# TensorE's order in a step of attention: scores, transposes, mixing, values

## The chip, the cores and the metric

The kernel runs on one core of one Trainium2 chip. The metric is the device time of one execution in microseconds (us), from the start of the program to its end. A core has a matrix engine (TensorE, PE in the rows), a vector engine (VectorE, DVE), an engine for functions of one argument (ScalarE, ACT), a general engine (GpSimd, POOL) and an engine that issues transfers (SyncE, SP). Each works through its own list of instructions and waits on semaphores for the others. PEld in the rows is TensorE's loading of the operand that stays in the array.

## What is computed

Attention with a bias made by a small network from the positions, then a dense layer with a softmax, a normalisation and a second matrix, then a mixture of eight experts with two experts per token. Only the attention is touched:

```python
def _attn_ref(q, k, v, w1, b1, w2):            # B 2, H 8, S 576, D 64; hidden 32
    scores = scale * np.matmul(q, k.transpose(0, 1, 3, 2))
    x = (psi_rel / psi_i)[..., None]           # from the positions alone
    h = np.maximum(x @ w1 + b1, 0.0)
    bias = h @ w2
    scores = scores + bias.transpose(2, 0, 1)[None]
    scores = scores - np.max(scores, axis=-1, keepdims=True)
    attn = np.exp(scores)
    attn = attn / (np.sum(attn, axis=-1, keepdims=True) + 1e-09)
    return np.matmul(attn, v)
```

## The kernel before

Attention is cut into 40 pieces A[k]: five tiles of queries (`it`, four of 128 rows and a last one of 64), four pairs of heads (`hp`) and two batches (`b`), with `b` running fastest. Two pieces that differ in `b` alone are a unit (`it`, `hp`); an even k is batch 0 of a unit, an odd k batch 1. A loop over k = 0, 1, 2, ... makes one step of each; what one piece needs is spread over several steps.

- **Scores**, `qk(k)` (L302, L306 for the last tile): TensorE multiplies queries and keys of two heads into two pairs of banks named `d`, one pair for each head. VectorE then adds the bias tile `bt`, which was brought from memory, and takes the extreme of each row in one instruction for each head (L311, output `e` and `nm`); it frees the bank. ScalarE takes the exponential of each head and the row sums (L318, output `e` and `sums`).
- **Transposes**, `tr(k - 2)` (LAG is 2): TensorE transposes `e` of the piece two steps back, eight blocks into one `d` (L330) and the remainders into `rest` (L332). ScalarE copies the blocks out (L333, output `et`), and for batch 1 the remainders of both batches (L335). For batch 1, VectorE makes the reciprocals `rs` of the sums (L337, L338), and GpSimd spreads them to `rb` (L341).
- **Values**, `av`: TensorE transposes `rb` (L353) and multiplies `et` with the values (L362) into the one bank `av`. ScalarE copies the product out (L365), VectorE multiplies it with the reciprocals (L366, output `XA`). Before, this is done for both batches of a unit at once, in every even step.
- **Mixing**, `bias_step` (L203): TensorE mixes 0/1 masks `mk` into the bias of positions that later pieces need, 16 matmuls into each of two `d`; VectorE frees them (L208 and L209) and SyncE stores the result. The masks are made by GpSimd (five of eight) and VectorE (three of eight) at L191. Twelve of the 36 mixing steps lie ahead of the loop, one in each step k = 0 to 23, none later.
- **Conversions**: the weights `w_in` and `w_out` come as 64-bit numbers, and from about step 20 on ScalarE (L252, L258), VectorE (L253, L255 to L257) and GpSimd (L253, L259) turn them into pairs of 32-bit numbers, in the gaps of attention.

There are three `d` (of two banks each); `rest` and `av` have one bank each. A step with mixing uses five `d`: one for transposes, two for scores, two for mixing. So each use waits until the use three before it has been emptied.

The program text gives the order of work; a scheduler then places each instruction on its engine's list by its own estimate of when operands are ready, so instructions can stand ahead of or behind their place in the text. On one engine nothing is reordered after that.

Of the kernel before, what the change touches and what calls it, by code (L numbers as in the profile page):

```python
# [9 lines left out]
F32 = mybir.dt.float32  # L10
# [10 lines left out]
B, H, S, D = 2, 8, 576, 64  # L21
# [5 lines left out]
JB = 5  # L27
# [5 lines left out]
LAG = 2  # L33
# [38 lines left out]
def _build(tc, nc, ctx, I, O):  # L72
# [267 lines left out]
                u.rb = ap.tile([128, 4, 64], F32, name="rb", bufs=2)  # L340
                P_.tensor_copy(u.rb, u.rs[:, :, None].to_broadcast([128, 4, 64]))  # L341

    def av(it, hp):

        u = SU.pop((it, hp))
        n = 128 if it < 4 else 64
        o = psum.tile([128, 2, 256], F32, name="av").rearrange("p w (b i) -> p w b i", b=2)
        for b in range(B):
            for x in range(2):
                h = slice(64 * x, 64 * x + 64)  # L350
                if n == 128:
                    if x == 0:
                        nc.tensor.transpose(o[:, 1, b], u.rb[:, 2 * b:2 * b + 2].rearrange("p x d -> p (x d)"), ident)  # L353
                else:
                    nc.tensor.matmul(o[h, 1, b, 0:64], u.rs[h, b:b + 1].to_broadcast([64, 64]), ident[h, h],
                                     start=True, stop=True)
        for b in range(B):
            v = KV[hp, b][:, S:].rearrange("p (j d) -> p j d", j=JB)
            for jb in range(JB):
                for x in range(2):  # L360
                    w = u.et[:, 2 * b + x, jb] if n == 128 else u.et[:, b, jb, 64 * x:64 * x + 64]
                    nc.tensor.matmul(o[64 * x:64 * x + 64, 0, b, 0:n], v[:, jb, 64 * x:64 * x + 64], w,  # L362
                                     start=(jb == 0), stop=(jb == JB - 1))
        dst = XA[:, it:it + 5:4, hp] if n == 128 else XA[:, 8, hp].rearrange("p (b i) -> p b i", b=2)
        nc.scalar.activation(dst, o[:, 0, :, 0:n], AF.Copy)  # L365
        V.tensor_tensor(out=dst, in0=dst, in1=o[:, 1, :, 0:n], op=OP.mult)  # L366
# [9 lines left out]
    for k in range(len(A) + LAG + 8):  # L376
        if k % 2 == 0 and k < len(A):
            bias_in(k // 2 + 2)
        if k % 8 == 6 and k // 8 + 1 < 5:
            load_q(k // 8 + 1)  # L380
        if LAG <= k < len(A) + LAG:
            tr(*A[k - LAG])
        if LAG <= k - 1 < len(A) + LAG and A[k - 1 - LAG][2] == 1:
            av(*A[k - 1 - LAG][:2])
        if k < len(A):
            qk(*A[k])
        bias_step(2 * PRE + k)
        if k == CONV[0] - 10:
            raws = [fetch_in(*c) for c in chunks[:RB64]]
        if k in CONV:  # L390
# [543 lines left out]
```

## Time and profile before

| | us |
|---|---|
| median of 3 runs | 640.64 |
| lowest and highest run | 640.61, 641.03 |
| the profiled execution | 641.07 |
| its span, first to last instruction | 639.3 |

The times of rows below are of the profiled execution and count from the start of its span. The masks and the first mixing steps take it to about 35 us; attention's loop then runs to about 237 us; the dense layer and the experts follow and are not touched. PEclk is the TensorE clock that was granted, as a share of full speed: 1.00 is 2.4 GHz and 0.50 is 1.2 GHz. In brackets behind an instruction stands how long its engine was idle just before it, and which instruction ended that wait. Instructions of one line that follow each other are merged, with their number behind the x; two on one engine can overlap by up to a tenth of a microsecond or so, since each is shown until its result has landed.

### The profile page before, as it was taken

The numbers are of one execution on the slowest core, as the hardware profiler recorded it, in microseconds if no ns is written. First come the engines' busy times: TensorE is split into PE (matmuls) and PEld (weight loads), VectorE is DVE, ScalarE is ACT, GpSimd is POOL, SyncE is SP. The second block draws the span as 40 slices with busy tenths as digits, with TensorE's granted clock in tenths as the row PEclk, the third lists the DMA queues.
The fourth block names the chain that finished last, engine by engine and source line by source line (L and its number), as shares of the span: only waits on it lengthen the run. The fifth ranks groups of instructions, "written<-read, shape, count | busy, mean of one in ns | idle before, by whom it ended". The sixth has DMA issues, their size and how long they took to land. (4 is left out here: it accounts for less than half of the span.)

```text
span 639.3 us, 12768 instructions
## 1 busy us (share of the span) xinstructions
PE 582.0 (91%) x5068; PEld 475.9 (74%) x5068; DVE 392.2 (61%) x909; ACT 341.9 (53%) x657; POOL 232.9 (36%) x177
## 2 busy tenths in 40 slices
PE   0879999998789999999999989999999999999990
PEld 0546777776567878678888788888898989898980
DVE  4988777777873336983546788774646474543400
ACT  6934656566675665663436436554545454544410
POOL 4999998973230017420000302322222121222111
PEclk9979999999989999999999999999999999999996
DMA  8794524317441015200312334757565656636212
GB/s 314 275 328 145 208 87 183 112 38 266 164 156 48 1 42 204 74 19 32 106 59 91 108 122 160 255 139 216 162 199 182 184 194 162 224 64 191 35 19 29
DMA packets 33945, 89.45 MB, mean 140 GB/s; under 512 B 3601, under 2 KB 5137, under 8 KB 33873
## 3 DMA queue, kind: packets, MB, share of 16 engines
q1 hardware_dynamic: 26480, 72.04, 31.3%
q0 software_dynamic: 5808, 13.37, 10.3%
q10 hardware_dynamic: 1584, 3.11, 1.3%
q8 instruction: 42, 0.69, 0.4%
q14 instruction: 31, 0.25, 0.1%
HBM read 67.66 MB, written 20.84 MB: 138 GB/s over the span
## 5 line engine op out<-in xcount | busy, mean ns | idle before, releaser
L191 POOL TENSOR_SCALAR mk<-T,thr 128x576 bf16<-128x576 f16 x67 | 116.9, 1759 | 13.0 <-PE d L203 8.9
L804 PE MATMUL phe<-xgt,wp 128*128 128x320 f32 x768 | 115.9, 310 | 2.3 <-ACT xgt L402 2.3
L804 PEld LDWEIGHTS phe<-xgt,wp 128*128 128x128 f32 x768 | 113.2, 188 | 3.0 <-ACT xgt L402 2.5
L638 POOL DMA_INDIRECT out<-y,si x24 | 39.6, 1652 | 149.5 <-ACT y L794 72.6
L787 PE MATMUL poe<-wp,hT 128*128 128x512 f32 x384 | 90.9, 393 | 0.0
L787 PEld LDWEIGHTS poe<-wp,hT 128*128 128x128 f32 x384 | 71.0, 188 | 14.1
L318 ACT ACTIVATE e<-e,nm 128x576 f32<-128x576 f32 x72 | 55.4, 771 | 42.5 <-DVE nm L311 42.4
L203 PE MATMUL d<-mk,wd 128*32 128x288 bf16 x1152 | 48.7, 302 | 26.9 <-POOL wd L170 14.2
L203 PEld LDWEIGHTS <-wd 128*32 128x32 f16 x1152 | 29.9, 100 | 47.3 <-issue 23.6
L311 DVE CUSTOM_DVE_ANT_0 e<-d,bt 128x576 f32<-128x576 f32 x72 | 52.2, 755 | 19.7 <-PE d L302 13.8
L807 DVE SCALAR_TENSOR_TENSOR hT<-phe,hT 128x320 fp32r<-128x320 f32 x64 | 31.3, 489 | 50.2 <-ACT hT L806 49.7
L302 PE MATMUL d<-kv,q 64*128 64x288 f32 x256 | 51.0, 447 | 5.7 <-DVE nm L311 5.2
L403 DVE TENSOR_TENSOR wp<-w2raw,wp 128x1024 fp32r<-128x1024 f32 x32 | 39.2, 1227 | 18.7 <-ACT wp L402 16.8
L806 ACT ACTIVATE hT<-phe 128x320 fp32r<-128x320 f32 x64 | 28.0, 437 | 41.3 <-PE phe L804 41.3
L362 PE MATMUL av<-et,kv 128*64 128x128 f32 (+1 forms) x800 | 46.1, 267 | 0.0
L666 POOL DMA_INDIRECT xg<-x1d,gi x21 | 21.7, 1032 | 61.4 <-DVE si L628 45.3
L362 PEld LDWEIGHTS av<-et,kv 128*64 128x64 f32 x800 | 41.0, 138 | 3.7 <-issue 3.3
L330 PE MATMUL d<-ident,e 128*128 128x128 f32 x288 | 40.8, 283 | 2.8 <-ACT et L333 1.7
L302 PEld LDWEIGHTS d<-kv,q 64*128 64x128 f32 x256 | 30.2, 193 | 17.2 <-DVE nm L311 6.9
L333 ACT ACTIVATE et<-d 128x1024 f32<-128x1024 f32 (+1 forms) x40 | 37.2, 931 | 9.6 <-PE d L330 9.4
L330 PEld LDWEIGHTS d<-ident,e 128*128 128x128 f32 x288 | 32.0, 143 | 13.4 <-DVE nm L311 7.8
L449 PE MATMUL ps<-mk,xs 128*128 128x512 f32 x162 | 40.5, 397 | 0.9 <-ACT xs L443 0.9
(194 smaller groups left out, 972.1 us busy)
## 6 DMA issues: line engine op xcount, KB each, us to landing
wraw<-moe_w SPq DMA_DIRECT2D x32, 512.0 KB, 7.6
w2raw<-moe_w SPq DMA_DIRECT2D x32, 512.0 KB, 6.4
biasd<-t SPq DMA_DIRECT2D x18, 576.0 KB, 4.2
bt<-biasd SPq DMA_DIRECT2D x16, 576.0 KB, 7.0
kv<-kv SPq DMA_DIRECT2D x8, 608.0 KB, 10.0
raw<-w_in SPq DMA_DIRECT2D x8, 512.0 KB, 7.7
raw<-w_out SPq DMA_DIRECT2D x8, 512.0 KB, 3.7
q<-q SPq DMA_DIRECT2D x5, 512.0 KB, 3.5
```

Source lines behind the costliest of these rows:

```text
L191: (V if e == "D" else P_).tensor_scalar(dst, w, thr[:, 0, q:q + 1], None, op0=OP.is_gt)
L203: nc.tensor.matmul(ps[32 * u:32 * u + 32, half, 0:288], WD[n][:, 32 * a:32 * a + 32], mk[:, 4 * gg + u, half * 288:half * 288 + 288], star ...
L302: nc.tensor.matmul(ss[x][:, a, 0:288], Q[it][h, n], k[h, a * 288:a * 288 + 288], start=True, stop=True)
L311: V.tensor_tensor_reduce(out=e.rearrange("p (a b) -> p a b", a=2), in0=ps[:, :, 0:288], in1=BT[it, hp][:, x].rearrange("p (a b) -> p a b", ...
L318: nc.scalar.activation(e, e, AF.Exp, bias=nm, scale=-1.0, accum_out=u.sums[:, c + x:c + x + 1])
L330: nc.tensor.transpose(pt[:, x, jb], e[:, jb * 128:jb * 128 + 128], ident)
L362: nc.tensor.matmul(o[64 * x:64 * x + 64, 0, b, 0:n], v[:, jb, 64 * x:64 * x + 64], w, start=(jb == 0), stop=(jb == JB - 1))
L403: return a, V.tensor_tensor(out=lo, in0=src, in1=hi.bitcast(F32), op=OP.subtract)
L449: nc.tensor.matmul(ph[:, a], xs[wx][:, k], WI[k, a][ww], start=(k == 0 and n == 0), stop=(k == 3 and n == 2))
L638: nc.gpsimd.indirect_dma_start(out=dst, out_offset=bass.IndirectOffsetOnAxis(ap=si, axis=0), in_=y, in_offset=None, compute_op=OP.add, bou ...
L787: nc.tensor.matmul(po, hT[f][wh][:, j:j + R], W2[f // 2][ww_][:, c:c + N], start=(f == 0 and m == 0), stop=(f == 7 and m == 2))
L804: nc.tensor.matmul(ph[:, 0:CAP], w1[k][ww_][:, f * 128:f * 128 + 128], xt[wx][:, k], start=(k == 0 and n == 0), stop=(k == 3 and n == 2))
```

## The change

The order of the calls in a step becomes scores, transposes, mixing, values. `av` gets the batch as an argument: each step does the values of one piece, A[k - 4], where before every even step did both batches of the unit whose second transposes were made in the step before. The copy out of the bank `av` and the product (L366 and L367 of the new text) still come once for a unit, after batch 1.

```diff
-    def av(it, hp):
-        u = SU.pop((it, hp))
+    def av(it, hp, b):
+        u = SU[it, hp] if b == 0 else SU.pop((it, hp))
...
-        o = psum.tile([128, 2, 256], F32, name="av").rearrange("p w (b i) -> p w b i", b=2)
-        for b in range(B):
+        if b == 0:
+            u.o = psum.tile([128, 2, 256], F32, name="av").rearrange("p w (b i) -> p w b i", b=2)
+        o = u.o
...
+        if b == 0:
+            return
         dst = XA[:, it:it + 5:4, hp] if n == 128 else XA[:, 8, hp].rearrange("p (b i) -> p b i", b=2)
...
+        if k < len(A):
+            qk(*A[k])
         if LAG <= k < len(A) + LAG:
             tr(*A[k - LAG])
-        if LAG <= k - 1 < len(A) + LAG and A[k - 1 - LAG][2] == 1:
-            av(*A[k - 1 - LAG][:2])
-        if k < len(A):
-            qk(*A[k])
         bias_step(2 * PRE + k)
+        if LAG + 2 <= k < len(A) + LAG + 2:
+            av(*A[k - LAG - 2])
```

No instruction of TensorE, VectorE, ScalarE, GpSimd or SyncE is added or taken away. Where each now stands on its engine, at three places:

**TensorE, steps 2 and 3, the first with transposes.** `kv_104` and `kv_106` are the keys of pieces 2 and 3. Before:

```order
L330 MATMUL d<-ident,e 128x128 x8
L332 MATMUL rest<-ident,e 128x128 x2
L302 MATMUL d<-kv_104,q 128x288 x4
...
L330 MATMUL d<-ident,e 128x128 x8
L332 MATMUL rest<-ident,e 128x128 x2
L302 MATMUL d<-kv_106,q 128x288 x4
...
L330 MATMUL d<-ident,e 128x128 x8
L332 MATMUL rest<-ident,e 128x128 x2
L353 MATMUL av<-ident,rb 128x128 x2
L362 MATMUL av<-et,kv_100 64x128 x10
```

and after (at the marks stand the 32 mixing matmuls of a step):

```order
L302 MATMUL d<-kv_104,q 128x288 x4
L330 MATMUL d<-ident,e 128x128 x8
L332 MATMUL rest<-ident,e 128x128 x2
...
L332 MATMUL rest<-ident,e 128x128 x2
L351 MATMUL av<-ident,rb 128x128
L302 MATMUL d<-kv_106,q 128x288 x4
L330 MATMUL d<-ident,e 128x128 x8
...
L332 MATMUL rest<-ident,e 128x128 x2
L302 MATMUL d<-kv_108,q 128x288 x4
```

The first transpose of `rb` stood behind the transposes of step 4; the scheduler now puts it ahead of the scores of step 3. On GpSimd the first copy to `rb` stands behind the same 26 masks in both kernels.

**VectorE, an odd step with mixing.** Before:

```order
L311 ISA e,nm<-d,bt 128x576
L311 ISA nm 128x1
L208 SCALAR_TENSOR_TENSOR t<-L,sp,d 128x576
L191 TENSOR_SCALAR mk<-T,thr 128x576
L209 SCALAR_TENSOR_TENSOR t<-d,unscale,t 128x576
L337 TENSOR_SCALAR rs<-sums 128x4
L191 TENSOR_SCALAR mk<-T,thr 128x576
L338 RECIPROCAL rs<-rs 128x4
L191 TENSOR_SCALAR mk<-T,thr 128x576
L366 TENSOR_TENSOR XA<-XA,av 128x2x128
L311 ISA e,nm<-d,bt 128x576
```

and after:

```order
L311 ISA e,nm<-d,bt 128x576
L311 ISA nm 128x1
L337 TENSOR_SCALAR rs<-sums 128x4
L208 SCALAR_TENSOR_TENSOR t<-L,sp,d 128x576
L338 RECIPROCAL rs<-rs 128x4
L191 TENSOR_SCALAR mk<-T,thr 128x576
L209 SCALAR_TENSOR_TENSOR t<-d,unscale,t 128x576
L191 TENSOR_SCALAR mk<-T,thr 128x576 x2
L367 TENSOR_TENSOR XA<-XA,av 128x2x128
L311 ISA e,nm<-d,bt 128x576
```

The instruction on `sums` (L337), which reads the sums of the pieces whose scores this very step and the one before have made, moved from behind both L208 and L209 to ahead of them. The product into `XA` stays ahead of the next step's L311.

**ScalarE, two steps with mixing**, odd then even. Before:

```order
L318 ACTIVATE e,sums<-e,nm 128x576 x2
L333 ACTIVATE et<-d 128x2x512
L365 ACTIVATE XA<-av 128x2x128
L318 ACTIVATE e,sums<-e,nm 128x576 x2
L333 ACTIVATE et<-d 128x2x512
L335 ACTIVATE et<-rest 128x4x128
```

and after:

```order
L318 ACTIVATE e,sums<-e,nm 128x576 x2
L333 ACTIVATE et<-d 128x2x512
L335 ACTIVATE et<-rest 128x4x128
L366 ACTIVATE XA<-av 128x2x128
L318 ACTIVATE e,sums<-e,nm 128x576 x2
L333 ACTIVATE et<-d 128x2x512
```

The copy L333 behind the two exponentials of a step now belongs to the transposes that TensorE makes right behind that step's scores; before, to those that it made after the mixing, at the start of the next step.

## Rows read from the trace of the kernel before

**Rows 1.** Page, part 1: engine, busy us, share of the span, instructions.
```profile
PE 582.0 (91%) x5068; PEld 475.9 (74%) x5068; DVE 392.2 (61%) x909; ACT 341.9 (53%) x657; POOL 232.9 (36%) x177
```
**Rows 2.** Windows: stretch, length, busy us by engine, PEclk, DMA share, GB/s.
```profile
57.36:141.98 84.62, 82.55 (x1140) 62.50 (x1136) 62.01 (x145) 49.10 (x95) 74.28 (x51) 1.00 0.36 131
141.98:167.94 25.96, 20.86 (x285) 15.84 (x285) 21.83 (x47) 17.05 (x35) 5.93 (x6) 1.00 0.57 203
167.94:189.26 21.32, 17.51 (x157) 13.11 (x157) 15.63 (x35) 15.59 (x30) 8.97 (x8) 0.94 0.52 169
189.26:208.09 18.83, 17.52 (x157) 14.23 (x157) 8.28 (x26) 11.58 (x25) 0.80 (x2) 0.89 0.20 66
208.09:237.28 29.19, 29.14 (x368) 23.86 (x368) 10.00 (x33) 17.75 (x41) 0.40 (x1) 1.00 0.06 20
```
**Rows 3.** Timeline, TensorE, one pair of steps: start us, us, instruction, [wait].
```profile
99.67 1.09 PE L330 MATMUL d<-ident,e 128*128 128x128 f32 x8
...
100.82 0.38 PE L353 MATMUL av<-ident,rb 128*128 128x128 f32 x2
...
103.46 1.24 PE L302 MATMUL d<-kv,q 64*128 64x288 f32 x8
...
105.56 0.68 PE L203 MATMUL d<-mk,wd 128*32 128x288 bf16 x16 [0.25 <-DVE nm L311]
106.24 1.09 PE L330 MATMUL d<-ident,e 128*128 128x128 f32 x8
...
107.48 1.64 PE L302 MATMUL d<-kv,q 64*128 64x288 f32 x8
109.05 1.19 PE L203 MATMUL d<-mk,wd 128*32 128x288 bf16 x32
110.25 1.09 PE L330 MATMUL d<-ident,e 128*128 128x128 f32 x8
```
**Rows 4.** Timeline, VectorE, from an odd step's scores to the next step's.
```profile
98.17 0.76 DVE L311 CUSTOM_DVE_ANT_0 e<-d,bt 128x576 f32<-128x576 f32 x1 [0.92 <-PE d L302]
...
99.53 0.81 DVE L208 SCALAR_TENSOR_TENSOR t<-L,sp,d 128x576 f32<-128x576 f32 x1
...
101.83 0.76 DVE L191 TENSOR_SCALAR mk<-T,thr 128x576 bf16<-128x576 f16 x1
...
104.00 0.42 DVE L366 TENSOR_TENSOR XA<-XA,av 128x256 f32<-128x256 f32 x1 [1.41 <-ACT XA L365]
104.74 0.76 DVE L311 CUSTOM_DVE_ANT_0 e<-d,bt 128x576 f32<-128x576 f32 x1 [0.32 <-PE d L302]
```
**Rows 5.** Timeline, ScalarE, a step without mixing or conversions.
```profile
197.05 0.78 ACT L318 ACTIVATE e<-e,nm 128x576 f32<-128x576 f32 x1 [1.57 <-DVE nm L311]
...
198.49 0.19 ACT L318 ACTIVATION_READ_ACCUMULATOR e<-e,nm 128x1 f32 x1
198.59 1.00 ACT L333 ACTIVATE et<-d 128x1024 f32<-128x1024 f32 x1
```
**Rows 6.** Timeline, GpSimd, from 18.91 us to the first `rb`.
```profile
18.91 38.70 POOL L191 TENSOR_SCALAR mk<-T,thr 128x576 bf16<-128x576 f16 x22 [0.62 <-ACT mk L189]
57.56 0.39 POOL L341 COPY rb<-rs 128x256 f32<-128x256 f32 x1
```
**Rows 7.** Timeline, TensorE, step 3 and the start of step 4.
```profile
54.28 2.05 PE L302 MATMUL d<-kv,q 64*128 64x288 f32 x8
...
57.36 1.09 PE L330 MATMUL d<-ident,e 128*128 128x128 f32 x8
...
58.51 0.38 PE L353 MATMUL av<-ident,rb 128*128 128x128 f32 x2
```
**Rows 8.** Timeline, TensorE, two long waits and a short one, steps 20 to 29.
```profile
149.87 0.68 PE L203 MATMUL d<-mk,wd 128*32 128x288 bf16 x16 [2.25 <-DVE nm L311]
...
186.36 2.96 PE L302 MATMUL d<-kv,q 64*128 64x288 f32 x8 [2.19 <-DVE nm L311]
...
199.64 1.09 PE L330 MATMUL d<-ident,e 128*128 128x128 f32 x8 [0.66 <-ACT et L333]
```
**Rows 9.** Windows: the granted clock (PEclk) around the second of those waits.
```profile
184.00:186.00 2.00, 0.17 (x2) 0.00 (x0) 2.00 (x4) 0.00 (x0) 1.29 (x1) 1.00 0.00 0
...
188.00:190.00 2.00, 2.00 (x9) 1.09 (x7) 1.96 (x4) 1.99 (x3) 0.00 (x0) 0.50 0.72 215
...
192.00:194.00 2.00, 2.00 (x25) 2.00 (x26) 0.00 (x0) 0.71 (x1) 0.00 (x0) 0.66 0.94 299
```

More of the change, by code (lines that the diff above doesn't have):

```diff
@@ L341, in tr @@
                 P_.tensor_copy(u.rb, u.rs[:, :, None].to_broadcast([128, 4, 64]))
-    def av(it, hp):
-        u = SU.pop((it, hp))
+    def av(it, hp, b):
+        u = SU[it, hp] if b == 0 else SU.pop((it, hp))
         n = 128 if it < 4 else 64
-        o = psum.tile([128, 2, 256], F32, name="av").rearrange("p w (b i) -> p w b i", b=2)
-        for b in range(B):
+        if b == 0:
+            u.o = psum.tile([128, 2, 256], F32, name="av").rearrange("p w (b i) -> p w b i", b=2)
+        o = u.o
+        if n == 128:
+            nc.tensor.transpose(o[:, 1, b], u.rb[:, 2 * b:2 * b + 2].rearrange("p x d -> p (x d)"), ident)
+        else:
             for x in range(2):
                 h = slice(64 * x, 64 * x + 64)
[L351 to L363, printed above, removed]
+                nc.tensor.matmul(o[h, 1, b, 0:64], u.rs[h, b:b + 1].to_broadcast([64, 64]), ident[h, h],
+                                 start=True, stop=True)
+        v = KV[hp, b][:, S:].rearrange("p (j d) -> p j d", j=JB)
+        for jb in range(JB):
+            for x in range(2):
+                w = u.et[:, 2 * b + x, jb] if n == 128 else u.et[:, b, jb, 64 * x:64 * x + 64]
+                nc.tensor.matmul(o[64 * x:64 * x + 64, 0, b, 0:n], v[:, jb, 64 * x:64 * x + 64], w,
+                                 start=(jb == 0), stop=(jb == JB - 1))
+        if b == 0:
+            return
         dst = XA[:, it:it + 5:4, hp] if n == 128 else XA[:, 8, hp].rearrange("p (b i) -> p b i", b=2)
```

## The prediction

> **What bounds the kernel now.** I read the page's busy shares first: TensorE is busy for 91% of the span [rows 1], so a step gets shorter only where TensorE waits. The windows over the attention loop show where that is [rows 2]. From step 4 to step 19 TensorE is busy for 82.55 of 84.62 us; in steps 20 to 23, with mixing and conversions, for 20.86 of 25.96; then for 17.51 of 21.32 and 17.52 of 18.83, both with a clock below 1.00; in the last tile for 29.14 of 29.19, so nothing is to be had there. Next I read one pair of steps on TensorE [rows 3]: it lasts 110.25 - 99.67 = 10.58 us. Two stalls show in it. The scores of the even rest take 1.64 instead of 1.24, because their second bank is freed late (0.40), and the second half of a mixing waits 0.25 for VectorE. Without both the pair would take 9.93.
>
> Then I followed one step around the engines, since each use of a `d` bank waits for the use three before it. Scores take 1.24 [rows 3]; L311 starts 0.04 later, takes 0.76 [rows 4], and the exponential of the first head starts 0.04 behind it. From that start to the end of the copy L333 it is 198.59 + 1.00 - 197.05 = 2.54, and the sums can be read 198.49 + 0.19 - 197.05 = 1.63 behind it [rows 5]. TensorE goes on 0.05 behind the copy (199.64) [rows 8]. So from the start of the scores it is 1.28 + 0.80 + 2.54 + 0.05 = 4.67 to a `d` freed by L333, if VectorE is free at 1.28. Before, that copy belongs to transposes made after the mixing, and nothing waits for it; in the new lists it frees the bank of the next scores. 4.67 is just below half of 9.93, so all hangs on VectorE.
>
> **Part 1, the start.** The new list has the first transpose of `rb` ahead of the scores of step 3. GpSimd makes that `rb` only behind its 26 masks, of which the last 22 run without a gap from 18.91 to 57.56 [rows 6]; that list is unchanged, so `rb` is there at 57.95. TensorE has then nothing it may do: before, it started the scores of step 3 at 54.28, step 4 at 57.36, and met `rb` only at 58.51, when it was ready [rows 7]. After, the scores of step 3 start at 58.0 and by the chain those of step 4 at 58.0 + 4.7 = 62.7. All work ahead of step 4 is the same in both, so this loses 62.7 - 57.36 = 5.3. Before, TensorE had done by 54.28 all that now stands ahead of the `rb`, and a group of transposes (1.1) besides [rows 3, 7]; so it now gets there near 52.5 and sits idle for 5 to 6 us. After a wait of 2.19 the scores took 2.96 instead of 1.24 [rows 3, 8], and the clock stood at 0.50, back only at about 193 [rows 9]. I add the scores' 1.7: **+7.0**, bounds +5.3 and +8.
>
> The Trainium skill bears on this. TensorE: Matmul & The Clock Gate, section "HAM oscillation — how this bites in real kernels", says that work after a long enough idle gap of TensorE begins at the low clock; it speaks against this change. By it the start costs 7.0; were the clock to stay up, 5.3. The trace agrees once (2.19, then 0.50) and not always: the wait of 2.25 at 149.87 was followed by full speed [rows 2, 8].
>
> **Part 2, steps 4 to 19, eight pairs.** In an odd step VectorE now meets L337 right behind its two L311. L337 needs the sums of this same step, there at 1.28 + 0.80 + 1.63 = 3.71; before, it stood where they were long made. Behind it are queued L208, which frees the first mixing bank, three masks, L209, and the product into `XA`; then the next step's L311. From L208 to the end of the last mask it is 101.83 + 0.76 - 99.53 = 3.06, the product is 0.42 [rows 4]. So the next L311 starts at 3.71 + 3.06 + 0.42 = 7.1 to 7.2 (0.1 less if they overlap). TensorE has started the even scores at 4.9 and would have had L311 go at 6.2: VectorE is late by 0.9. The even step's L333 ends at 7.1 + 0.80 + 2.54 = 10.4, and the next odd scores start at 10.5. The even step's mixing gives the same: both L311 take 99.53 - 98.17 = 1.36 [rows 4], to 8.5; then half a mixing (0.6) and half the values (1.3 of 103.46 - 100.82) [rows 3] bring TensorE to 10.4. So the pair stays where it was, 10.5 against 10.58: the two stalls of before go, and one for VectorE takes their place. The first even step has no such step ahead of it: 4.8 + 7 x 10.5 + 4.9 = 83.2 against 84.62, **-1.4**. Bounds: -5.4 if pairs run at 9.93 (4.8 + 69.5 + 4.9), +1.5 if at 10.9. I take the chain's value because all its durations are rows.
>
> GpSimd needs five masks of about 1.76 (38.70 / 22) [rows 6] and one `rb` of 0.39, 9.2 a pair, and stays below 10.5; its `rb` is now used a whole mixing later. SyncE's list keeps its order but for a few `w_out` loads beside bias tiles of the last tile, hidden by the steps between issue and use. That `av` is begun in one step and ended in the next keeps its one bank for longer; the next unit's first values come three matmul groups later, behind the copy and product: nothing.
>
> **Part 3, steps 20 to 23, with conversions.** In both lists ScalarE's conversions stand behind a step's copies and ahead of the next exponentials, and VectorE's first conversion ahead of the next L311. So the wait of 2.25 for L311 [rows 8] stays; it only moves to the first half of the mixing. **-0.4**; bounds -4.1 (VectorE is busy for 21.83 of the 25.96 [rows 2]) and +2 (that wait once more).
>
> **Part 4, steps 24 to 27** (to 189.26). No mixing; transposes wait for L333 two steps back. The wait of 2.19 ahead of the scores of step 27 is for L311 [rows 8]; one piece's values (1.3) now stand ahead of every step's scores there, so I take half of it as filled. With the clock then up, 1.7 of scores and 1.1 of wait: **-2.8**; bounds -5.7 (VectorE busy for 15.63) and +1.
>
> **Part 5, steps 28 to 31** (to 208.09). TensorE's own work for a pair is 9.93 less two mixings of 1.19 = 7.5; VectorE's product is still ahead of the next L311, some 0.4 more: two pairs 15.8 against 18.83, **-3.0**. Bounds -3.8 (7.5 alone) and -1.3 (17.52 busy, the low clock kept).
>
> **The last tile and all behind it**: 0, bounds half a us either way. The lists behind attention are the same, so they shift.
>
> **Sum.** 7.0 - 1.4 - 0.4 - 2.8 - 3.0 = -0.6 against the profiled execution's 641.07, so 640.5 there. The median of the runs lies 0.43 below that execution: **640.0**.
>
> **Rivals.**
> 1. *Slower, 644: the clock falls in steps 20 to 23.* By hand I get waits of TensorE of 2.0 at step 20 and 1.8 at step 22, for L311 behind conversions. The row of 2.25 without a fall speaks against it, that of 2.19 with one for it. It decides when one such wait is followed by 0.50. Price: some 7 us at half speed [rows 9], 3.5 lost, and 0.5 of part 4 not gained.
> 2. *Faster, 635: VectorE is in time.* If VectorE's odd step is 0.6 shorter than I add up, because masks and product overlap more, the pair goes to 9.93: seven pairs give 4.0, part 5 another 0.8. Against it stands that no mask in rows 4 is shorter than what I used.
> 3. *Slower, 647: nothing comes back.* The start is lost, pairs stay at 10.58, the conversions hold parts 3 and 4 where they were (or 0.7 above), and part 5 gives its least: 640.64 + 7.0 - 1.3 + 0.7 = 647.0.
> 4. *Faster, 633: the start is not lost*, because TensorE passes over the transpose that waits for `rb`: 7.0 less. In the trace later matmuls do stand behind a mixing that waits 2.25 [rows 8]. PSUM — Partial Sum Buffer, section "Engine vs sequencer instructions", of the Trainium skill says that matmuls start in program order; by that the time is 640.0, without it 633.0, and the trace agrees with the page.
>
> **How the numbers follow.** Forecast (638.3 to 642): 0.40. Rival 1: 0.27, rival 2: 0.20, rival 3: 0.08, rival 4: 0.05. A measurement of this kernel tells 0.2% (1.3 us) from no change, so "same" is 639.36 to 641.92. Faster: rivals 2 and 4 and a third of the forecast, 0.38. Same: most of the forecast and the mildest of rival 1, 0.30. Slower: 0.32. The range, 634.8 to 645.2, leaves out rivals 3 and 4 and a little of each end.
>
> **What would show it.** Right: TensorE idle from 52 or 53 to 58 us with GpSimd's `rb` as what ends it; the next scores at about 3 us; L337 waiting about 1.0 for ScalarE in every odd step; even L311 some 0.9 behind their scores; pairs of 10.4 to 10.6 with the stall now ahead of mixing or odd scores and L333 or L311 as its end; no clock of 0.50 between 185 and 200. Wrong: pairs of 9.9 or of 11; a window with PEclk 0.5 around 150 to 175; or that gap missing.

## The result and the profile after

| | median | runs | lowest to highest |
|---|---|---|---|
| before | 640.84 us | 4 | 640.61 to 642.08 |
| after | 648.74 us | 4 | 647.93 to 649.77 |

The new order is slower: ratio 1.012, 95% interval 1.0097 to 1.0143. The median lies above the prediction of 640.0 and above the end of its range, 645.2. The profiled execution of after took 648.51 us with a span of 646.7; that of before had a span of 639.3, so 7.4 us have to be found.

The windows of the kernel after, cut at the same points of the work as [rows 2] (start of step 4, 20, 24, 28, 32, end of the last values); columns as there:

```profile
64.63:148.94 84.31, 81.71 (x1135) 60.73 (x1134) 61.46 (x145) 47.03 (x96) 71.80 (x49) 1.00 0.34 126
148.94:174.34 25.40, 20.91 (x286) 15.35 (x284) 21.72 (x46) 16.21 (x33) 5.75 (x6) 1.00 0.61 225
174.34:197.35 23.01, 19.07 (x158) 14.51 (x157) 15.66 (x37) 15.22 (x32) 9.21 (x8) 0.85 0.54 178
197.35:212.88 15.53, 15.18 (x158) 11.77 (x157) 7.19 (x23) 11.70 (x25) 0.80 (x2) 1.00 0.07 20
212.88:243.12 30.24, 29.54 (x370) 23.98 (x368) 9.68 (x32) 16.98 (x39) 0.40 (x1) 1.00 0.06 20
```

Against before that makes this account (a step starts with its transposes before, with its scores after; the last tile is counted here to the first matmul of the dense layer, at 238.13 before and 244.01 after):

| part | before | after | difference | predicted |
|---|---|---|---|---|
| 1, start of step 4 | 57.36 | 64.63 | +7.3 | +7.0 |
| 2, steps 4 to 19 | 84.62 | 84.31 | -0.3 | -1.4 |
| 3, steps 20 to 23 | 25.96 | 25.40 | -0.6 | -0.4 |
| 4, steps 24 to 27 | 21.32 | 23.01 | +1.7 | -2.8 |
| 5, steps 28 to 31 | 18.83 | 15.53 | -3.3 | -3.0 |
| last tile | 30.04 | 31.13 | +1.1 | 0 |
| behind attention | 401.17 | 402.69 | +1.5 | 0 |
| sum | | | +7.4 | -0.6 |

**The start.** Timeline of TensorE, kernel after (start us, us, instruction, wait and its releaser), which answers to [rows 7]:

```profile
51.85 0.44 PE L332 MATMUL rest<-ident,e 128*128 128x128 f32 x2
57.76 0.48 PE L351 MATMUL av<-ident,rb 128*128 128x128 f32 x1 [5.47 <-POOL rb L341]
58.17 2.29 PE L302 MATMUL d<-kv,q 64*128 64x288 f32 x8
60.39 1.97 PE L330 MATMUL d<-ident,e 128*128 128x128 f32 x8
62.29 2.04 PE L203 MATMUL d<-mk,wd 128*32 128x288 bf16 x32
...
64.63 1.25 PE L302 MATMUL d<-kv,q 64*128 64x288 f32 x8
```

TensorE is done at 52.3, waits 5.47 us for GpSimd's first `rb`, and then runs scores, transposes and mixing at nearly double their usual 1.24, 1.09 and 1.16. The window from 58 to 64 has a granted clock of 0.50, that is 1.2 of 2.4 GHz. This is the gap that was predicted, at the predicted place and size.

**A pair of steps.** TensorE and then VectorE in the kernel after, around steps 12 and 13, which answers to [rows 3, 4]:

```profile
106.28 1.24 PE L302 MATMUL d<-kv,q 64*128 64x288 f32 x8
...
109.16 1.35 PE L203 MATMUL d<-mk,wd 128*32 128x288 bf16 x32 [0.39 <-DVE nm L311]
...
111.94 1.24 PE L302 MATMUL d<-kv,q 64*128 64x288 f32 x8
...
116.95 1.24 PE L302 MATMUL d<-kv,q 64*128 64x288 f32 x8
```
```profile
105.08 0.17 DVE L337 TENSOR_SCALAR rs<-sums 128x4 f32<-128x4 f32 x1 [1.09 <-ACT e L318]
105.16 0.81 DVE L208 SCALAR_TENSOR_TENSOR t<-L,sp,d 128x576 f32<-128x576 f32 x1
...
108.02 0.41 DVE L367 TENSOR_TENSOR XA<-XA,av 128x256 f32<-128x256 f32 x1
108.35 0.74 DVE L311 CUSTOM_DVE_ANT_0 e<-d,bt 128x576 f32<-128x576 f32 x1
```

The pair lasts 116.95 - 106.28 = 10.67 (10.58 before). L337 waits 1.09 for ScalarE with L208 behind it, and the even step's L311 starts 2.07 behind its scores, where the odd one has 1.27 (113.21 against 111.94).

**Steps 25 to 27.** TensorE, then ScalarE, then VectorE in the kernel after, which answers to [rows 8, 9]:

```profile
183.85 1.65 PE L302 MATMUL d<-kv,q 64*128 64x288 f32 x8
187.69 1.97 PE L330 MATMUL d<-ident,e 128*128 128x128 f32 x8 [2.20 <-ACT et L333]
189.46 0.64 PE L332 MATMUL rest<-ident,e 128*128 128x128 f32 x2
190.67 0.45 PE L351 MATMUL av<-ident,rb 128*128 128x128 f32 x1 [0.58 <-DVE XA L367]
191.05 2.40 PE L361 MATMUL av<-et,kv 128*64 128x128 f32 x20
193.38 1.45 PE L302 MATMUL d<-kv,q 64*128 64x288 f32 x8
```
```profile
184.02 0.68 ACT L252 ACTIVATE t<-raw 128x512 f32<-128x512 f32 x1 [1.82 <-POOL t L259]
...
185.11 0.77 ACT L318 ACTIVATE e<-e,nm 128x576 f32<-128x576 f32 x1
...
186.63 1.01 ACT L333 ACTIVATE et<-d 128x1024 f32<-128x1024 f32 x1
```
```profile
186.31 1.48 DVE L255 TENSOR_SCALAR t<-t 128x512 uint32<-128x512 uint32 x1 [2.11 <-POOL t L253]
...
189.46 0.73 DVE L311 CUSTOM_DVE_ANT_0 e<-d,bt 128x576 f32<-128x576 f32 x1
```

The wait of 2.19 of before is not gone; it stands one step earlier, as one of 2.20, and the low clock stands behind it again (0.50 in the window from 188 to 192). The wait that ends it is now one for ScalarE. ScalarE is held at L252, the first step of converting the output weights, until GpSimd is done with L259; the exponentials, whose input VectorE had finished at 183.5, stand behind it and start at 185.11, and L333 behind them. That ScalarE's, VectorE's and GpSimd's queues are strictly first in, first out is what the Trainium skill says (PSUM — Partial Sum Buffer, section "Engine vs sequencer instructions"); the rows agree, by 1.6 us here.

VectorE is late as well, and sets the end of the delay. Its L255 waits 2.11 for GpSimd's L253, which itself could start only behind ScalarE's L252; the L311 of step 26 and the product L367 stand behind it, and TensorE waits for that product again, 0.58 at 190.67. The transposes and remainders between the two waits are 0.88 and 0.26 longer than usual by the low clock, and that is 1.1 less of the second wait: in the second profile of this kernel, further down, they run at full speed and the second wait is 1.67. TensorE is idle for 23.01 - 19.07 = 3.94 us in steps 24 to 27, where before it was 21.32 - 17.51 = 3.81.

**The end.** In the last tile TensorE meets one wait that before did not have. Behind attention it meets one that before had too, ahead of the first matmuls of the experts, but this time the work behind it is slower. Two rows of the kernel after, then the second of them in the kernel before:

```profile
241.06 0.33 PE L355 MATMUL av<-ident,rs 64*64 64x64 f32 x4 [0.70 <-DVE XA L367]
...
385.16 8.74 PE L806 MATMUL phe<-xgt,wp 128*128 128x320 f32 x48 [2.27 <-ACT xgt L404]
```
```profile
379.29 7.27 PE L804 MATMUL phe<-xgt,wp 128*128 128x320 f32 x48 [2.26 <-ACT xgt L402]
```

The granted clock is 0.50 from 386 to 388 us in the kernel after, and 0.91 on the mean of the stretch from 140 to 160 us behind the dense layer's first matmul; in the kernel before it is 1.00 throughout that stretch. The 48 matmuls lose 8.74 - 7.27 = 1.5 us by it. This is called the dip below.

### The profile page after: what moved, and what is told of

Its sections match the earlier page's. It is cut to its first block, busy times and chain, and to the rows that moved or that the text cites. A ratio compares the mean times of both kernels' runs of the same rounds, so it can differ in the third digit from the quotient of the medians.

```text
span 646.7 us, 12781 instructions
## 1 busy us (share of the span) xinstructions
PE 585.0 (90%) x5068; PEld 475.6 (74%) x5068; DVE 390.1 (60%) x909; ACT 338.3 (52%) x657; POOL 231.9 (36%) x177
## 4 chain that ended last, share of the span: by engine, by line
PE 63%; DVE 12%; ACT 7%; issue 6%; DMA 5%; POOL 4%; POOLq 0%; DVEq 0%; ACTq 0%
PE phe L806 16%; PE poe L789 11%; PE ps L451 6%; PE av L361 4%; PE poe L793 4%; ACT e L318 3%; PE av L490 3%; DMA out<-y,si 3%; PE d L302 3%; PE d L203 3%; DVE e L311 3%; PE pt L490 3%; PE d L330 2%; PE d L306 1%; POOL mk L191 1%
## 5 line engine op out<-in xcount | busy, mean ns | idle before, releaser
L806 PE MATMUL phe<-xgt,wp 128*128 128x320 f32 x768 | 117.4, 312 | 2.3 <-ACT xgt L404 2.3
L806 PEld LDWEIGHTS phe<-xgt,wp 128*128 128x128 f32 x768 | 114.7, 190 | 3.0 <-ACT xgt L404 2.5
L311 DVE CUSTOM_DVE_ANT_0 e<-d,bt 128x576 f32<-128x576 f32 x72 | 51.8, 751 | 34.2 <-PE d L302 23.7
L203 PEld LDWEIGHTS <-wd 128*32 128x32 f16 x1152 | 31.3, 102 | 40.9 <-issue 16.7
L361 PE MATMUL av<-et,kv 128*64 128x128 f32 (+1 forms) x800 | 49.5, 271 | 0.0
L302 PE MATMUL d<-kv,q 64*128 64x288 f32 x256 | 45.1, 449 | 4.1 <-DVE nm L311 2.3
L404 ACT ACTIVATE wp<-w2raw 128x1024 fp32r<-128x1024 f32 x32 | 33.9, 1061 | 13.0 <-DMA w2raw<-moe_w 6.3
L333 ACT ACTIVATE et<-d 128x1024 f32<-128x1024 f32 (+1 forms) x40 | 36.7, 921 | 7.2 <-PE d L330 7.2
```

Source lines behind the costliest of these rows:

```text
L203: nc.tensor.matmul(ps[32 * u:32 * u + 32, half, 0:288], WD[n][:, 32 * a:32 * a + 32], mk[:, 4 * gg + u, half * 288:half * 288 + 288], star ...
L302: nc.tensor.matmul(ss[x][:, a, 0:288], Q[it][h, n], k[h, a * 288:a * 288 + 288], start=True, stop=True)
L311: V.tensor_tensor_reduce(out=e.rearrange("p (a b) -> p a b", a=2), in0=ps[:, :, 0:288], in1=BT[it, hp][:, x].rearrange("p (a b) -> p a b", ...
L806: nc.tensor.matmul(ph[:, 0:CAP], w1[k][ww_][:, f * 128:f * 128 + 128], xt[wx][:, k], start=(k == 0 and n == 0), stop=(k == 3 and n == 2))
```

## The experiments

Each ratio is to the kernel before, run beside it on the same chip; there the kernel before had medians of 640.9 to 642.4, so ratios are safer to compare than times. The kernel after has 1.012.

### The start: the first `rb` by VectorE

```diff
-                P_.tensor_copy(u.rb, u.rs[:, :, None].to_broadcast([128, 4, 64]))
+                (V if (it, hp) == (0, 0) else P_).tensor_copy(u.rb, u.rs[:, :, None].to_broadcast([128, 4, 64]))
```

> The new order, but the copy rb of the first unit alone is made by VectorE instead of GpSimd, so that it need not stand behind the masks. Theory (the start is lost to that rb): TensorE no longer idles 5.5 us ahead of 57.8, no low clock follows it, the scores of step 4 start at 57.4 to 58.5 instead of 64.63, and the time falls by 6 to 7.3 us, from 648.7 to between 641.4 and 642.7. Rival (something else, the bias tiles or the masks themselves, holds the start of the new order): scores of step 4 not before 62, gain under 3 us.

643.16 us, ratio 1.0021 (0.9998 to 1.0045): 1.0% of the 1.2% are gone. TensorE in this kernel:

```profile
51.60 0.27 PE L351 MATMUL av<-ident,rb 128*128 128x128 f32 x1
52.49 1.75 PE L302 MATMUL d<-kv,q 64*128 64x288 f32 x8 [0.62 <-ACT et L333]
...
57.51 1.79 PE L302 MATMUL d<-kv,q 64*128 64x288 f32 x8 [0.29 <-DVE t L208]
```

The gap is gone, and step 4 starts at 57.51 instead of 64.63, 7.1 earlier. So the start is lost to that one copy. The median is 0.5 above the expected range; in the profile steps 24 to 27 lose 1.6 of the 7.1 again, to a low clock that lasts longer there (24.59 us at 0.79).

### L337 behind L209

Each L337 gets an order behind the L209 of the odd step in which it stood (MX holds them by number of mixing).

```diff
+            s = 2 * PRE + 8 * it + 2 * hp + 1
+            with tc.issue_after(MX[min(s, 2 * NM - 1)]):
-            V.tensor_scalar(u.rs[:, 0:2 * n], u.sums[:, 0:2 * n], 1e-9, None, op0=OP.add)
+                V.tensor_scalar(u.rs[:, 0:2 * n], u.sums[:, 0:2 * n], 1e-9, None, op0=OP.add)
```

> The new order, but VectorE's L337 (sums) and L338 are held in its list behind the L209 of the same step, where they no longer stop L208. Theory (the wait of 1.09 of L337 for ScalarE makes the even L311 late and keeps the pair of steps at 10.66): the pair falls to 10.0 to 10.2, steps 4 to 19 from 84.3 to 80 to 81 us, the time from 648.7 to 644.5 to 645.5. Rival (VectorE is late anyway, or the copy L333 and the bank it frees hold the pair): pair 10.5 or more, steps 4 to 19 at 83.5 or more, time 648.

647.24 us, ratio 1.0087 (1.0069 to 1.0106). The pair falls only to 130.69 - 120.35 = 10.34, about half of what was expected, and the time is 1.7 above the expected range. VectorE and TensorE in this kernel (L313 is L311 of before, L304 the scores, L371 the product):

```profile
125.36 1.24 PE L304 MATMUL d<-kv,q 64*128 64x288 f32 x8
```
```profile
126.77 0.41 DVE L371 TENSOR_TENSOR XA<-XA,av 128x256 f32<-128x256 f32 x1
127.11 0.74 DVE L313 CUSTOM_DVE_ANT_0 e<-d,bt 128x576 f32<-128x576 f32 x1
```

L337's wait was half of the matter. The even L313 is still 1.75 behind its scores, 0.5 late, with VectorE's product right ahead of it: without the wait the odd step's list is still too long.

### Both edits

> Both edits together: the first rb by VectorE, and L337 behind L209 in every step. If the two costs are separate they add: 648.7 - 6.5 - 3.7 = 638.5, between 637.4 and 639.5, below the kernel before. If a VectorE that is earlier in steps 4 to 19 only hands its time to the conversions of steps 20 to 27: 641 or more.

640.42 us, ratio 0.9970 (0.9948 to 0.9993), 0.9 above the expected range. Within the intervals the two gains add: 1.0 and 0.3% alone, 1.5% together (1.0120 to 0.9970). The new order is now no slower than the old one, but steps 24 to 31 still take 40.17 us in its profile (of the slowest of its ten executions, 643.18), against 40.15 before.

### The old order up to step 27, the new from 28 on

```diff
+        new = k >= 28
-        if k < len(A):
+        if new and k < len(A):
             qk(*A[k])
         if LAG <= k < len(A) + LAG:
             tr(*A[k - LAG])
+        if not new:
+            if k % 2 == 0 and 0 <= k - LAG - 2 < len(A):
+                av2(*A[k - LAG - 2][:2])
+            if k < len(A):
+                qk(*A[k])
         bias_step(2 * PRE + k)
-        if LAG + 2 <= k < len(A) + LAG + 2:
+        if new and LAG + 2 <= k < len(A) + LAG + 2:
             av(*A[k - LAG - 2])
```

(av2 is `av` of before.)

> The order of before up to step 27, the new order from step 28 on. In the new kernel steps 28 to 31 took 3.3 us less than before. Theory A (2.3 of that is only that the low clock fell and ended earlier there, in steps 24 to 27): with the old steps 24 to 27 the low clock reaches into step 28 again, steps 28 to 31 gain 1 us, the last tile loses up to 1 us to the split values, and the time is 640 to 641. Theory B (the new order itself is worth the 3.3 us): steps 28 to 31 take 15.5 us, time 637.5 to 638.5.

641.06 us, ratio 1.0000 (0.9982 to 1.0018). The time is theory A's, but the profile does not decide:

```profile
187.17 1.91 PE L302 MATMUL d<-kv,q 64*128 64x288 f32 x8 [2.21 <-DVE nm L311]
```
```profile
188.00:190.00 2.00, 1.97 (x10) 1.12 (x11) 1.97 (x4) 2.00 (x5) 0.00 (x0) 1.00 0.29 55
```

The wait is that of before (2.21, and 2.19 in [rows 8]), and this time the clock stayed at 1.00. Steps 28 to 31 took 15.92, without a low clock, so this run cannot divide the difference to 18.83 between clock and order; the rows of the kernel before can, under part 5 below. The last tile took 31.13, as after. What the run shows is that the same wait has both outcomes, and that behind it the scores take 1.91 at full clock, where [rows 8] has 2.96.

### The output weights later, after and before

The first conversion instruction of each output weight is put behind the exponentials of step 28 in ScalarE's list (EX holds them).

```diff
-        for g in f64_parts(raws.pop(0), *WO[f], *CO[f]):
+        first, *rest = f64_parts(raws.pop(0), *WO[f], *CO[f])
+        with tc.issue_after(EX[28]):
+            first()
+        for g in rest:
             g()
```

> The new order; the first conversion of the output weights (L252, into t64) is held in ScalarE's list until the exponentials of step 28. In the new kernel that L252 stood ahead of the exponentials of step 25 and waited 1.82 us for GpSimd's L259. Theory (that instruction makes L333 late, TensorE waits 2.20 for it at 187.69, and the low clock behind the wait costs 2.6 more): the wait falls under 0.8, no clock of 0.50 follows, steps 24 to 31 go from 38.5 to 33.5 to 35 us, the time from 648.7 to 644 to 645. Rival (VectorE's conversions of the input weights hold these steps anyway): a wait over 1.5 stays, the low clock too, time 647.5 or more.

646.21 us, ratio 1.0082 (1.0054 to 1.0110). TensorE and VectorE in this kernel:

```profile
186.19 1.09 PE L330 MATMUL d<-ident,e 128*128 128x128 f32 x8 [0.65 <-ACT et L333]
...
201.82 1.91 PE L302 MATMUL d<-kv,q 64*128 64x288 f32 x8 [1.02 <-DVE nm L311]
```
```profile
200.27 0.83 DVE L255 TENSOR_SCALAR t<-t 128x512 uint32<-128x512 uint32 x1 [4.14 <-POOL t L253]
201.02 0.74 DVE L311 CUSTOM_DVE_ANT_0 e<-d,bt 128x576 f32<-128x576 f32 x1
```
```profile
174.37:192.73 18.36, 16.53 (x159) 12.41 (x157) 11.22 (x31) 14.09 (x30) 6.28 (x6) 1.00 0.50 166
192.73:211.67 18.94, 16.20 (x159) 12.08 (x157) 10.68 (x30) 13.36 (x27) 4.15 (x5) 1.00 0.23 72
```

Of the wait of 2.20 are 0.65 left, the transposes behind it take 1.09, and steps 24 to 27 fall from 23.01 to 18.36 with the clock at 1.00: that the conversion of the output weights makes the delay in part 4 is confirmed. The edit moves all links of that chain at once, so it does not tell L252's hold on ScalarE from L255's on VectorE. And steps 28 to 31 rise from 15.53 to 18.94. The conversion now does there what it did before: VectorE's L255 waits for GpSimd's L253, and L311 stands behind it. Together they take 37.30, where 33.5 to 35 were expected, and the time is 1.2 above its range. Of the 4.7 us gained 1.2 are left at the end of attention (the dense layer starts at 242.81, after at 244.01).

> The kernel before with the same edit alone. Theory: its wait of 2.19 at 186.36 was also for the output weights (VectorE's L255 waited 2.67 for two L253 on GpSimd, with L311 behind it), so wait and low clock go: steps 24 to 31 from 40.2 to 34 to 36 us, the time from 641.5 to 636 to 637.5. If the wait is due to the bank or to the exponentials of the step itself: 641 and no change.

643.67 us, ratio 1.0034 (1.0012 to 1.0057): missed. Step 27 loses its wait (0.65 for L333 is left there), so that wait did belong to this conversion; but step 31 gets one, where the scores at 203.54 wait 2.44 for L311 and take 2.96. Its dense layer starts at 238.11, to 0.02 where it did before. Its profiled execution is 1.8 longer, and 1.7 of that lies behind attention, where it has the dip; whether that also makes the median 0.3% higher is not shown.

> The new order with three edits together: first rb by VectorE, L337 behind L209, and the output weights' L252 behind the exponentials of step 28. If the costs are separate: 640.4 of the first two less 4 to 5, 635 to 637, below the kernel before by 0.7 to 1.0%, and at the level of the kernel before with the edit of the output weights. If the low clock only falls at another place: 639 or more.

639.19 us, ratio 0.9953 (0.9931 to 0.9975). That is 2 above the expectation. Steps 24 to 27 took 18.74, but steps 28 to 31 took 18.93, with VectorE's conversion waiting 4.13 for GpSimd: more than half of the gain (24.64 to 18.74 in the first four steps, 15.53 to 18.93 in the next) was handed on to the same conversion, four steps later.

### And its L253 on VectorE

```diff
-    CO = [(P_, P_)] * 4 + [(V, P_)] * 4
+    CO = [(V, P_)] * 2 + [(P_, P_)] * 2 + [(V, P_)] * 4
```

> As the version with three edits (first rb by VectorE, L337 behind L209, output weights' L252 behind the exponentials of step 28), and the L253 of the two output-weight conversions that run inside attention goes from GpSimd (1.49 each, two in a row) to VectorE (0.41 to 0.8). There the conversions had only moved the stall: VectorE's L255 waited 4.14 for GpSimd's L253 with L311 behind it, and steps 28 to 31 took 18.9. Theory (the stall is that in-order wait for GpSimd): steps 28 to 31 take 15.5 to 16.5, the time falls from 639.2 to 635.5 to 637. Rival (any conversion in these steps costs its VectorE time on the path): 18 or more, 639.

636.68 us, ratio 0.9937 (0.9917 to 0.9956). The time is in the expected range. Steps 28 to 31 took 17.25, 1.7 less than with L253 on GpSimd, but 0.8 above the expected range. Of the 3.4 that the conversions cost in these steps (18.93 against 15.53 with none there) half is gone with the wait for GpSimd; the other half stays, with TensorE waiting 0.41 to 0.66 for ScalarE's copies (L333 of before) in three of the four steps. Steps 24 to 31 together take 35.99, against 38.54 after.

> The kernel before with the same two edits of the output weights: L252 behind the exponentials of step 28, and L253 of the first two on VectorE. With the first edit alone the wait of 2.19 at step 27 had turned into one of 2.44 at step 31. Theory: that wait goes too, steps 24 to 31 take 34 to 36 instead of 40.2, time 636 to 637.5. If the wait goes and the time stays at 640 or above, the gain is given back behind attention.

638.60 us, ratio 0.9962 (0.9938 to 0.9985). From the scores of step 24 to those of step 32 it takes 36.0 us instead of 40.2 in the old order, as expected; the time is 1.1 above the expected range. Of the 4.2 us steps 20 to 23 give 1.5 back (27.41 at a clock of 0.94, 25.95 at 1.00 before): the wait of 2.25 in step 20 is the same as in [rows 8], and this time the low clock came behind it.

### VectorE's product behind the next L311

```diff
-        V.tensor_tensor(out=dst, in0=dst, in1=o[:, 1, :, 0:n], op=OP.mult)
+        LATE.append(lambda: V.tensor_tensor(out=dst, in0=dst, in1=o[:, 1, :, 0:n], op=OP.mult))
         ...
             qk(*A[k])
+        for late in LATE:
+            with tc.issue_after(NM_[0]):
+                late()
+        LATE.clear()
```

(NM_[0] is the last L311 issued.)

> As the version with four edits, and VectorE's product into XA goes behind the two L311 of the next even step. With L337 behind L209 the pair was still 10.34, and even L311 started 0.5 late, right behind the product. Theory (VectorE's list in the odd step holds the pair): the pair falls by 0.25 to 0.34, to 10.0 to 10.1, and the time by 1.5 to 2.5 to 633.5 to 635. Rival (the product then holds L208 and the av bank, and the wait moves there): pair 10.3 or more.

634.03 us, ratio 0.9893 (0.9854 to 0.9933).

```profile
108.82 1.24 PE L304 MATMUL d<-kv,q 64*128 64x288 f32 x8
...
118.83 1.24 PE L304 MATMUL d<-kv,q 64*128 64x288 f32 x8
```
```profile
58.27:138.87 80.60, 80.57 (x1133) 59.92 (x1134) 64.75 (x146) 47.54 (x97) 73.00 (x49) 1.00 0.38 139
```

The pair is 10.01, and TensorE is busy for 80.57 of 80.60: VectorE's list was all that held steps 4 to 19 (82.31 with the edits ahead of this one). Yet in these two profiles attention ends alike (dense layer at 232.42 and 232.29): step 4 starts 1.1 later here, for a reason not followed up, and steps 20 to 23 take 26.95, at a clock of 0.94, instead of 25.73 at 1.00. The spans differ by the dip behind attention, which only the earlier version's profile has; the intervals of the two ratios overlap.

### One part of the change alone

> One part of the change alone: scores ahead of the transposes, but the values of both batches every second step, behind the transposes, as before. TensorE's list has the first rb ahead of the scores of step 3 as in the new order. Theory (the start is lost by the scores' place, not by the split values): scores of step 4 not before 62 us, and the time is 646 to 650. Rival (the split of the values by batch is what costs): scores of step 4 at 58, time 640 to 642.

(The line order: scores, transposes, values of both batches every second step, mixing.) 650.76 us, ratio 1.0150 (1.0115 to 1.0186). `rb` is waited for 5.67 us and step 4 starts at 64.93.

> The other part of the change alone: the values split by batch and put at the end of each step, the transposes ahead of the scores as before. TensorE's list has the first rb behind the scores of step 4 again. Theory (the start is lost by the scores' place): scores of step 4 at 57 to 58.5. Each pair pays some 0.3 for the split values; steps 4 to 19 at 84 to 88, the last tile 30, time 641 to 645. If the split were what lost the start: scores of step 4 behind 62, time 647 or more.

(Transposes, scores, mixing, values of one batch.) 644.99 us, ratio 1.0057 (1.0032 to 1.0081). No gap; step 4 starts at 56.67, its scores at 57.92. So the start is lost by the place of the scores alone. In the loop each half costs: from the scores of step 4 to those of step 20 both kernels take 87.4 us, 10.9 a pair, against 10.66 with both. With the values alone each mixing waits 0.25 for L311 half way; with the scores alone their second bank is late in the odd step (0.33, for L208) and they wait 0.25 for L333 in the even one.

### The last tile in the old order

```diff
+        new = k < 32
```

(The rest as in the kernel with the new order from 28 on.)

> The new order up to step 31, the order of before from step 32 on (the last tile). In the new kernel the last tile took 31.1 us from the start of step 32 to the first matmul of the dense layer, against 30.0 before: 0.4 in matmuls split in two, 0.7 in a wait for VectorE's product. Theory (both come with the values split by batch): the last tile is back at 30.0 to 30.2, the time falls by 1.0. Rival (the last tile pays for the scores' place or for what came before): 31 again, no change.

648.72 us, ratio 1.0100 (1.0073 to 1.0127). Step 32 starts at 213.11 and the dense layer at 243.68: 30.57, half of the way from 31.13 to 30.04. The wait of 0.70 is gone; one of 0.23 at the change of order and scores in two pieces are there instead.

> As the version with the product behind L311 (five edits, 634.0), and the order of before from step 32 on. If the last tile's 1.1 us come with the split values: last tile 30.0 to 30.3 instead of 31.1, time 632.5 to 633.5. If not: 634.

633.86 us (631.68 to 635.08), ratio 0.9868 (0.9831 to 0.9905): 30.60 against 31.14 in its last tile, half again, and no difference to the version without this edit (0.9893) that can be measured. The two are the fastest of the study, 1.1 and 1.3% below the kernel before.

### The kernel after once more

> The new kernel once more, beside the two above. Behind attention the profiled executions so far take either 400.4 to 401.3 or 402.6 to 402.9 us, the longer with a clock of 0.91 in the stretch 140 to 160 us behind the dense layer's first matmul, in seven kernels out of fourteen and whatever the order in attention. If that is independent of the change, the time is 647.2 or 648.7 by which of the two comes, and this profile shows either; attention itself ends within 0.5 us of 244.0 in it. If the new order brings the dip: 402.7 and 648.7 again.

649.83 us, ratio 1.0116 (1.0085 to 1.0146). Behind attention 402.62, with the dip as in the first profile (0.91). But attention ended at 245.4 instead of 244.0, outside the 0.5 that was expected. 1.0 of these 1.4 us come from steps 24 to 27 (23.98 for 23.01): the clock fell at 189.5 instead of 187.0 and rose at 196.2 instead of 193.8.

Every one of the 17 profiles (one of each kernel, two of the kernel after) has the wait ahead of the experts' first matmuls, 2.26 or 2.27 us long. In 9 the low clock follows and the 48 matmuls take 8.74 to 8.82; in 8 it does not and they take 7.27 or 7.28. It comes in the old order (in the kernel with the first edit of the output weights, not in the kernel before and not in the one with both edits) as well as in the new. What decides it stays open. Both profiles of the kernel after have the dip and the one of the kernel before has not; so few cannot exclude that the new order makes it likelier.

## Why the prediction was wrong

The sum missed by 8.0 us: 4.5 in part 4, 1.1 each in part 2 and the last tile, 1.5 behind attention, and 0.3 at the start, less 0.5 in parts 3 and 5. With part 4 as forecast the median would have been 4.5 lower, 644.2, and inside the range.

**Part 1 was right**, in place, cause and size: +7.3 against +7.0, with 5.47 us of waiting, a clock of 0.50 behind it, and 7.1 back when the copy was moved. The Trainium skill (TensorE: Matmul & The Clock Gate, section "HAM oscillation — how this bites in real kernels") lets work after a long enough gap begin at the low clock; behind the wait of 5.47 the trace agrees. The size was helped by luck: the 1.7 added for the clock was read off the scores of 2.96, of which 1.91 - 1.24 = 0.7 is a bank that comes late at full clock too. Here the scores took only 1.05 longer, but transposes and mixing took 0.88 longer each, and from the scores of step 3 to those of step 4 it took 64.63 - 58.17 = 6.46, 1.8 more than the chain's 4.7.

**Part 2 had the right mechanism and too short a pair.** L337 waits 1.09, the even L311 is 0.8 late (0.9 predicted), and the pair ends up unchanged. It is 10.66 instead of 10.5: the late L311 makes the mixing wait 0.39 and take 1.35 instead of 1.16, and TensorE's own pair is 10.01, not 9.93. Seven pairs of 0.16 are the 1.1 us that are missing. That all hangs on VectorE was right: L337 and the product together are worth 10.66 - 10.01 a pair.

**Part 3 was right** (-0.6 against -0.4), with waits of 1.72 and 1.15 for L311 ahead of the mixing and one of 1.45 for L333 ahead of the scores of step 23.

**Part 4 is the step that failed**: +1.7 against -2.8, outside its bounds of -5.7 and +1. The prediction read "2.19 for L311" and filled half of that wait with values; it did not ask what VectorE was waiting for. Ahead of that L311 stood L255 of a conversion, which waited 2.67 until the first of two L253 on GpSimd was done. GpSimd and VectorE in the kernel before:

```profile
182.35 2.94 POOL L253 TENSOR_SCALAR t<-t 128x512 f32<-128x512 f32 x2 [0.59 <-ACT t L252]
...
183.87 0.83 DVE L255 TENSOR_SCALAR t<-t 128x512 uint32<-128x512 uint32 x1 [2.67 <-POOL t L253]
...
185.55 0.74 DVE L311 CUSTOM_DVE_ANT_0 e<-d,bt 128x576 f32<-128x576 f32 x1
```

The wait belonged to a chain over ScalarE, VectorE and GpSimd in queues that run in order, and such a chain goes with the conversion and not with TensorE's order: started later, it made its wait later, in both orders. In the new order another link of it, L252 behind L259, held ScalarE first, and L255 held VectorE as before. The forecast took 1.1 of TensorE's 3.81 idle us away; there were 3.94. With the wait came the low clock, which the prediction had taken away with it; it came in all six profiles of the new order in which this conversion is not moved (waits of 2.19 to 2.21, 23.0 to 24.8 us for steps 24 to 27). And of the 1.7 of scores to be gained by the clock only 2.96 - 1.91 = 1.05 was the clock's.

**Part 5 was right in size, half of it by luck** (-3.3 against -3.0). The low clock of before reached into these steps. TensorE in the kernel before, at the start of step 28:

```profile
189.26 0.69 PE L353 MATMUL av<-ident,rb 128*128 128x128 f32 x2
189.74 1.91 PE L330 MATMUL d<-ident,e 128*128 128x128 f32 x8
191.44 0.64 PE L332 MATMUL rest<-ident,e 128*128 128x128 f32 x2
192.00 3.04 PE L362 MATMUL av<-et,kv 128*64 128x128 f32 x40
```

Against 0.38, 1.09, 0.38 and 2.40 at full speed that is 0.31 + 0.82 + 0.26 + 0.64 = 2.0 us of the 17.52 in [rows 2]. The second pair of these steps ran at full clock and took 208.09 - 199.64 = 8.45 [rows 2, 8], so two would take 16.9: of the 3.3 some 1.9 is the clock and 1.4 the new order (15.53, against 15.8 forecast). The forecast had the clock up here because it took the wait ahead away; it was up because the low clock had come one step earlier.

After, the low clock was paid in part 4. By the rows above the matmuls took 0.88 + 0.26 + 0.18 + 1.09 + 0.21 = 2.6 longer, of which the first two, 1.1, only shortened the wait for VectorE behind them. So it cost about 1.5 after and about 1.05 + 1.9 = 3.0 before. Parts 4 and 5 together moved by -1.6 and were predicted at -5.8; by these estimates both kernels would take some 37.1 us for the eight steps at full clock. What the new order gained in part 5 it lost in part 4 to longer waits, and even the 1.6 is the clock's and not the order's.

**The last tile** was put at 0 and cost 1.1. The split values add 0.4 of busy time (29.54 against 29.14), and in the drain L355 waits 0.70 for VectorE's product. About half came back with the old order there; the rest stays unexplained.

**Behind attention** the 1.5 us are the low clock behind a wait that every kernel has there, which comes and goes in kernels of both orders. It is in the account because one execution is compared with another; the trace of before, where the same wait of 2.26 passed at full clock, gave a prediction no cost to put down to the change.

**The rivals.** The fourth (TensorE passes over the transpose) is excluded by the gap. The first had the low clock in steps 20 to 23, where it did not come, though three waits of 1.15 to 1.72 did; it came where the forecast had it removed. (In five of the experiments' profiles, among them the one with both edits of the output weights in the old order, it did come in steps 20 to 23.) The nearest was the third, 647 with a chance of 0.08: the start is lost and nothing comes back in the pairs and the conversions. That chance was too small, since it needed no mishap: only that the waits for conversions stay where the conversions are. Its 647 is near in part by luck: it had +6.4 up to step 31, where +4.8 was measured, and nothing for the last tile and the dip.

## What to carry to other kernels

Follow a wait through the queue of the engine that is named: what stands ahead of the late instruction there, and what does that wait for? A wait that comes from another job in an in-order queue does not go away when the waiting engine's order changes, and moving that job alone moves the stall with it (here from step 26 to step 30); taking the slow engine out of its chain removed half of what it cost. Before an instruction is moved ahead, look up when its first input is made: one copy that stood behind 26 masks cost 7 us here. And before a difference between two traces is put down to the change, take out what the clock did in each.

## What the runs showed of the hardware

The clock did not answer to a wait's length alone. In the kernels before and after it fell to 0.50 at a wait of TensorE of 2.19 or 2.20, in the first 0.2 us behind the wait's end, in the second 0.7 ahead of it. In the kernel with the new order from step 28 on, a wait of 2.21 was followed by 1.00 throughout. In the second profile of after the transposes behind 2.20 ran at full speed (1.09); the clock fell at 189.5, when a second wait had just begun, and the work behind that one was slow:

```profile
188.09 1.09 PE L330 MATMUL d<-ident,e 128*128 128x128 f32 x8 [2.20 <-ACT et L333]
...
191.07 0.45 PE L351 MATMUL av<-ident,rb 128*128 128x128 f32 x1 [1.67 <-DVE XA L367]
```

In step 20 of the old order a wait of 2.25 was followed by 1.00 in the kernel before, and by a mean of 0.57 from 150 to 154 us in the one with both edits of the output weights. Behind attention the same wait of 2.26 or 2.27 had the low clock behind it in 9 profiles of 17.

Where it came in steps 24 to 31, the low clock cost about 1.5 us after, 0.18 + 1.09 + 1.05 + 0.13 = 2.45 in the second profile of after (the excess of the four groups of matmuls behind the second wait), and about 3.0 before; the dip cost 1.5. So two executions of one program can differ by some us. The runs of one kernel lie 1 to 7 us apart, and the clock is a part of that: among the 25 runs of the kernel before beside the first experiments, time and mean granted clock go against each other (correlation -0.78; 639.42 us at 0.983, 643.94 at 0.974). It is not all: in the version with the first `rb` by VectorE ten runs lie 5.0 apart at clocks of 0.977 to 0.980, and what makes that is not shown.
